# A gated feed-forward layer on one core: both first x blocks in one transfer, and the transposing transfer behind two gate loads

## The chip, the cores and the metric

The kernel runs on one core of a Trainium2 chip. Times are microseconds of device time for one execution. The engines are TensorE (PE; PEld is its loading of weights), VectorE (DVE), ScalarE (ACT), GpSimd (POOL) and SyncE (SP). SP and ACT issue the DMA transfers, each on a queue of its own, and 16 DMA engines carry them out.

## The reference

```python
def reference(x, w_gate, w_up, w_down):
    return (_gelu(x @ w_gate) * (x @ w_up)) @ w_down
```

`x` is [32, 32, 1024] in bf16, so 1024 tokens of 1024 features; `w_gate` and `w_up` are [1024, 3584], `w_down` is [3584, 1024], all bf16, and `_gelu` is the tanh approximation.

## The kernel before

The kernel computes each of its large products in two halves of every dimension, with Strassen's scheme (Winograd's form): seven products of sub-matrices in place of eight, at the price of sums and differences that VectorE and GpSimd form. In the first phase the left operand is the pair (gate, up), cut by feature half: `a11` and `a12` are the gate's rows for the features 0 to 511 and 512 to 1023, `a21` and `a22` those of up. The right operand is x transposed, cut by feature half and token half: `b11`, `b12` (features 0 to 511, first and second 512 tokens), `b21`, `b22` (features 512 to 1023). Each of these tiles is 128 partitions by 4 blocks (`KD` = 4, a block k is 128 features) by 512 tokens. The second phase multiplies the result by `w_down` in the same way; the change doesn't touch it.

The products with `t1` to `t4` (differences of the b tiles) and `s1` to `s4` (sums of weight tiles) need many tiles before they can begin. The kernel therefore opens with products that need little: gate rows `a12` by `b21`, for the first 24 of 28 column blocks of 128 (`NAHEAD` = 24), in six groups of four (`KB` = 4). The gate rows of groups 0 and 1 go to the tiles `a12a`, those of groups 2 to 5 to the tiles `a12b`; one 128x512 product has four matmuls, k = 0 to 3. Its result is copied out of the accumulators to `ahead`.

The whole is written under a manual schedule: each engine and each queue does its work in the order of the program text, and semaphores hold an instruction until what it needs is there. A transfer also waits, on its issuing engine, until the transfer eight places before it in the program has landed, since eight semaphores are used in turn. So the order of the lines is the order of the queues.

For the change, the opening matters. `b21` must be filled with transposed x. Its blocks k = 0 and 1 come the quick way: x is loaded as it lies, into `x_nat` (`load_nat`, L200), TensorE transposes it by 128x128 blocks into accumulator tiles `tp` (L267), and a copy takes each `tp`, half of the tokens of one block, to `b21` (L270). Its blocks k = 2 and 3 come by a transposing DMA transfer, `load_xT` (L220). In the kernel before, the order of the transfers is:

- SP: `x_nat` block 0; gate row k = 0 of group 0; gate row k = 1 of group 0; the transposing transfer of `b21` blocks 2 and 3; gate rows 2 and 3 of group 0; of group 1; the `a12b` rows of groups 2 and 3; `wu` and `wg` of the first chunk of weights; the rows of group 4; `b11`; `b12`; and so on.
- ACT: a tiny load of gate values, `probe` (L209); `x_nat` block 1; gate rows 0 and 1 of group 1. Behind these ACT loads its activation table.

The order on TensorE is: six matmuls on constants (L259, `NWARM`), the four transposes of x block 0, four short matmuls on constants (L274, `NFILL`), then the products (L289). Group 0 with k = 0 is done for the first half of the tokens; then x block 1 is transposed; then k = 0 for the second half, k = 1 for the first and the second, all these as 16 matmuls of 256 columns. Group 1 with k = 0 and 1 follows (8 matmuls of 512 columns), then k = 2 and 3 of group 0 and of group 1, then the groups 2 to 5 and the rest of the kernel.

Of the kernel before, what the change touches and what calls it, by code (L numbers as in the profile page):

```python
# [13 lines left out]
def kernel(  # L14
# [20 lines left out]
    nc = tc.nc  # L35
    P = nc.NUM_PARTITIONS
# [6 lines left out]
    xf = x.flatten_outer_dims()  # L43
# [5 lines left out]
    DT, FT = D // P, F // P  # L49
    KD = DT // 2  # L50
# [4 lines left out]
    KQ = DT // 4  # L55
# [4 lines left out]
    KB = 4  # L60
# [47 lines left out]
    def acc(tag):  # L108
        return ps1.tile([P, NB], fp32, name=f"ps{tag}", tag=tag, bufs=BANKS[tag])
# [5 lines left out]
    b21 = xpool.tile([P, KD, NB], bf16, name="b21")  # L115
# [8 lines left out]
    ahead_at = [t[:, k, :] for t in ahead for k in range(t.shape[1])]  # L124
# [38 lines left out]
    def sums(ci, *engs):  # L163

        a11, a12, a21, a22 = quads(ci)
        s1, s2, s4, s3 = (
            spool.tile([P, KD, FC * P], f32r, name=n, tag=n)[:, :, : len(chunks[ci]) * P]
            for n in ("s1", "s2", "s4", "s3")
        )
        s_tiles[ci] = (s1, s2, s3, s4)  # L170
        yield engs[0].tensor_tensor(s1, a21, a22, ADD)  # L171
        yield engs[1].tensor_tensor(s2, s1, a11, SUB)  # L172
        yield engs[2].tensor_tensor(s4, a12, s2, SUB)  # L173
        yield engs[3].tensor_tensor(s3, a11, a21, SUB)  # L174
# [17 lines left out]
    NB_P = NB // P  # L192
    probe = xpool.tile([P // 8, KQ, 2], bf16, name="probe")
    nc.gpsimd.memset(probe, 0.0)  # L194
    HALF = NB_P // 2
    x_nat = spool.tile([P, NB_P, KQ * P], bf16, name="x_nat", tag="s1")

    with tc.manual_schedule():
        def load_nat(eng, dt, p0, p1):
            eng.dma_start(  # L200
                out=x_nat[:, p0:p1, dt * P : (dt + 1) * P],
                in_=xf[p0 * P : p1 * P, (KD + dt) * P : (KD + dt + 1) * P].rearrange("(b p) d -> p b d", p=P),
            )

        assert KQ == 2
        load_nat(nc.sync, 0, 0, NB_P)


        nc.scalar.dma_start(out=probe, in_=wg_r[::8, KD : KD + KQ, :2])  # L209

        def load_ahead(i, k0, k1, eng=nc.sync, j0=0, j1=KB):
            f0 = i * KB
            eng.dma_start(
                out=a12_ahead[i][:, k0:k1, j0 * P : j1 * P],
                in_=wg_r[:, KD + k0 : KD + k1, (f0 + j0) * P : (f0 + j1) * P],
            )

        def load_xT(nb, d0, d1):
            t = ((b11, b12), (b21, b22))[d0 // KD][nb]
            nc.sync.dma_start_transpose(  # L220
                out=t[:, d0 % KD : (d1 - 1) % KD + 1, :], in_=xf[nb * NB : (nb + 1) * NB, d0 * P : d1 * P]
            )

        load_ahead(0, 0, 1)
        load_nat(nc.scalar, 1, 0, NB_P)
        load_ahead(0, 1, 2)
        load_xT(0, KD + KQ, DT)
        load_ahead(1, 0, KQ, nc.scalar)
        a12_ahead += [spool.tile([P, KD, KB * P], bf16, name="a12b", tag=t) for t in ("s2", "s4", "s1", "s3")]
        for i in (0, 1):  # L230
            load_ahead(i, KQ, KD)
        def load_halves(i):
            for k in range(0, KD, KQ):
                load_ahead(i, k, k + KQ)

        load_halves(2)
        load_halves(3)
        for which in (1, 0):
            load_w_all(0, which)
# [20 lines left out]

        tps = [[ps1.tile([P, HALF * P], bf16, name="tp", tag="A", bufs=BANKS["A"]) for _ in range(2)] for _ in range(KQ)]

        def transposed(dt):
            for half, tp in enumerate(tps[dt]):
                p0 = half * HALF
                for b in range(HALF):
                    nc.tensor.transpose(  # L267
                        tp[:, b * P : (b + 1) * P], x_nat[:, p0 + b, dt * P : (dt + 1) * P], ident
                    )
                nc.vector.tensor_copy(b21[:, dt, p0 * P : (p0 + HALF) * P], tp)  # L270

        transposed(0)
        for _ in range(NFILL):
            nc.tensor.matmul(warm_ps[:, :P], lhsT=ones_w, rhs=ones_w, start=True, stop=True)  # L274

# [11 lines left out]
        def product_ahead(ps, i, j, k0=0, k1=KD, cols=slice(None)):  # L287
            for k in range(k0, k1):
                nc.tensor.matmul(  # L289
                    ps[:, cols],  # L290
                    lhsT=a12_ahead[i][:, k, j * P : (j + 1) * P],
                    rhs=b21[:, k, cols],
                    start=(k == 0 and not cols.start),
                    stop=(k == KD - 1),
                    skip_group_check=True,
                )

        def group_ahead(i, tags, copies=(nc.scalar.copy,), between=None):
            for j, tag in enumerate(tags):
                if between and 2 * j == KB:  # L300
                    between()
                ps = acc(tag)
                product_ahead(ps, i, j)
                copies[j % len(copies)](ahead_at[i * KB + j], ps)
# [22 lines left out]

        both = (nc.scalar.copy, nc.vector.tensor_copy)  # L330
        ps = [[acc(t) for t in tags] for tags in ("CCAA", "AAAA")]
        for k in range(KQ):
            for half in range(2):
                for j in range(KB):
                    product_ahead(ps[0][j], 0, j, k, k + 1, slice(half * HALF * P, (half + 1) * HALF * P))
                if k == half == 0:
                    transposed(1)
        for j in range(KB):
            product_ahead(ps[1][j], 1, j, 0, KQ)
        for i in (0, 1):  # L340
            for j in range(KB):
                product_ahead(ps[i][j], i, j, KQ)
                both[j % 2](ahead_at[i * KB + j], ps[i][j])
        group_ahead(2, "CCAA", both)
        group_ahead(3, "AAAA", both)
        chunk0 = sums(0, *[nc.gpsimd] * 3, nc.vector)
        for _ in range(3):
            next(chunk0)
# [241 lines left out]
        for h0, h1, upto in ((0, NB - P, NB // 2), (NB - P, NB, NB)):  # L590
            cols = slice(h0, h1)
            ps = acc("C")[:, : h1 - h0]
# [33 lines left out]
```

## Time and profile before

| what | value |
|---|---|
| time, median of three runs | 274.2 us (273.19, 274.2, 274.35) |
| span of the profiled execution, first to last instruction | 271.9 us |
| TensorE busy | 267.5 us, 98% |
| VectorE busy | 204.0 us, 75% |
| ScalarE busy | 115.5 us, 42% |
| GpSimd busy | 119.7 us, 44% |
| moved by DMA | 35.86 MB, mean 132 GB/s |
| granted TensorE clock, mean | 1.000 |

The profiled execution's own time is given by its span; the profile states no other time for it. The span leaves out what lies before the first and after the last instruction, so it is compared with spans, and the median with medians. In the profile, a group of instructions is named by its line, its engine, and "written tile<-read tiles"; numbers behind an arrow in square brackets are the idle time before it and what ended it. "Time to landing" of a transfer runs from the start of its issue to its last signal of completion.

### The profile page before, as it was taken

What the parts mean: (1) busy time and instruction counts of PE and PEld (TensorE: products, weight loads), DVE (VectorE), ACT (ScalarE), POOL (GpSimd) and SP (SyncE); (2) the same over time, 40 slices, a digit from 0 to 9 for tenths busy, and PEclk for the clock granted to TensorE, in tenths of its full rate; (3) what the DMA queues carried; (4) which work ended last, traced back from release to release, by engine and by line L of the source; (5) the groups of instructions that cost most, each with busy time, mean ns of one, the idle gap of its engine ahead of it and who ended that gap; (6) DMA issues with size and microseconds to landing.
All of it is one profiled execution on the core that took longest, in us unless ns stands there. A gap on an engine that the chain in (4) does not pass through costs nothing.

```text
span 271.9 us, 3424 instructions
## 1 busy us (share of the span) xinstructions
PE 267.5 (98%) x1216; PEld 192.9 (71%) x1216; DVE 204.0 (75%) x205; ACT 115.5 (42%) x189; POOL 119.7 (44%) x61
## 2 busy tenths in 40 slices
PE   7999999999999999999999999999999999999995
PEld 4444776886787688688688687764458888888883
DVE  1447998986976877876777478469999999998621
ACT  2335756545644653645636535434000307870000
POOL 1090089986994995995995987000000000000000
PEclk9999999999999999999999999999999999999999
DMA  6999321504505505415234190005981437774111
GB/s 162 328 237 233 84 78 39 158 25 130 157 0 154 155 2 154 121 33 157 69 88 120 43 333 9 0 2 189 359 262 60 164 106 261 260 214 156 66 50 58
DMA packets 56576, 35.86 MB, mean 132 GB/s; under 512 B 9840, under 2 KB 56560, under 8 KB 56560
## 3 DMA queue, kind: packets, MB, share of 16 engines
q1 hardware_dynamic: 53264, 33.17, 43.0%
q10 hardware_dynamic: 3296, 2.49, 2.8%
q8 instruction: 9, 0.15, 0.2%
q14 instruction: 7, 0.06, 0.1%
HBM read 31.72 MB, written 2.10 MB: 124 GB/s over the span
## 4 chain that ended last, share of the span: by engine, by line
PE 97%; DMA 1%; POOL 0%; issue 0%; DVE 0%; ACTq 0%; POOLq 0%
PE psA L278 38%; PE psA L430 24%; PE psC L278 19%; PE psC L430 7%; PE psA L289 5%; PE psC L289 2%; DMA x_nat<-in_x_dram 1%; PE psC L594 1%; PE tp L267 0%; POOL ident masks.py:199 0%; DVE o_last L595 0%; POOL probe L194 0%; ACTq L209 0%; POOL ident masks.py:197 0%; POOLq L610 0%
## 5 line engine op out<-in xcount | busy, mean ns | idle before, releaser
L278 PE MATMUL psA<-t,s 128*128 128x512 f32 x224 | 57.3, 397 | 0.0
L251 ACT ACTIVATE h<-c 128x512 bf16<-128x512 f32 x56 | 34.6, 629 | 41.4 <-DVE c L308 41.4
L278 PEld LDWEIGHTS psA<-t,s 128*128 128x128 f32 x224 | 42.1, 188 | 9.5
L171 POOL TENSOR_TENSOR s<-wu 128x1024 fp32r<-128x1024 bf16 x13 | 28.9, 2224 | 31.4 <-DMA wu<-in_w_up_dram 30.7
L172 POOL TENSOR_TENSOR s<-s,wg 128x1024 fp32r<-128x1024 f32 x14 | 32.0, 2286 | 15.3 <-DVE s L171 14.3
L278 PE MATMUL psA<-b,wg 128*128 128x512 bf16 x128 | 29.4, 380 | 0.0
L174 POOL TENSOR_TENSOR s<-wg,wu 128x1024 fp32r<-128x1024 bf16 x13 | 28.4, 2187 | 0.0
L278 PE MATMUL psA<-t,a22r 128*128 128x512 f32 x112 | 27.9, 391 | 0.0
L278 PE MATMUL psC<-t,s 128*128 128x512 f32 x112 | 27.9, 391 | 0.0
L278 PE MATMUL psC<-b22r,s 128*128 128x512 f32 x112 | 27.7, 389 | 0.0
L308 DVE TENSOR_TENSOR c<-sn,psA 128x512 f32<-128x512 f32 x32 | 21.8, 682 | 6.7 <-PE psA L278 5.9
L313 ACT COPY sn<-psC 128x512 f32<-128x512 f32 x28 | 16.3, 588 | 22.9 <-PE psC L278 15.2
L278 PEld LDWEIGHTS psC<-t,s 128*128 128x128 f32 x112 | 21.0, 188 | 4.5
L278 PEld LDWEIGHTS psA<-t,a22r 128*128 128x128 f32 x112 | 21.0, 188 | 4.5
L278 PEld LDWEIGHTS psC<-b22r,s 128*128 128x128 f32 x112 | 21.0, 188 | 4.4
L308 DVE TENSOR_TENSOR c<-sn,psC 128x512 f32<-128x512 f32 x28 | 19.2, 687 | 6.2 <-PE psC L278 6.2
L407 DVE TENSOR_TENSOR lo<-c,h 128x512 bf16<-128x512 f32 x14 | 22.5, 1608 | 0.9
L278 PEld LDWEIGHTS <-wg 128*128 128x128 bf16 x128 | 11.8, 98 | 15.3 <-issue 2.4
L173 POOL TENSOR_TENSOR s<-wg,s 128x1024 fp32r<-128x1024 bf16 x10 | 21.6, 2158 | 0.8
L313 ACT COPY sn<-psA 128x512 f32<-128x512 f32 x32 | 18.3, 592 | 4.9 <-PE psA L278 4.7
L308 DVE TENSOR_TENSOR c<-ahead,psA 128x512 f32<-128x512 f32 x24 | 16.4, 687 | 3.9 <-PE psA L278 2.3
L326 DVE TENSOR_TENSOR hi<-h,psA 128x512 bf16<-128x512 bf16 x14 | 9.6, 688 | 11.3 <-PE psA L278 11.3
(88 smaller groups left out, 381.0 us busy)
## 6 DMA issues: line engine op xcount, KB each, us to landing
wu<-in_w_up_dram SPq DMA_DIRECT2D x14, 512.0 KB, 4.0
wdb<-in_w_down_dram SPq DMA_DIRECT2D x12, 512.0 KB, 4.8
wg<-in_w_gate_dram SPq DMA_DIRECT2D x9, 512.0 KB, 5.3
wdb<-in_w_down_dram SPq DMA_DIRECT2D x12, 384.0 KB, 4.6
v<-in_w_down_dram SPq DMA_DIRECT2D x4, 512.0 KB, 6.4
out_dram<-o_sb ACTq DMA_DIRECT2D x15, 128.0 KB, 1.7
a12b<-in_w_gate_dram SPq DMA_DIRECT2D x6, 256.0 KB, 5.1
wg<-in_w_gate_dram SPq DMA_DIRECT2D x6, 256.0 KB, 4.7
```

Of the source, the lines that this page charges most:

```text
L171: yield engs[0].tensor_tensor(s1, a21, a22, ADD)
L172: yield engs[1].tensor_tensor(s2, s1, a11, SUB)
L173: yield engs[2].tensor_tensor(s4, a12, s2, SUB)
L174: yield engs[3].tensor_tensor(s3, a11, a21, SUB)
L251: nc.scalar.activation(h, src, ACT.Gelu_apprx_tanh)
L278: nc.tensor.matmul(ps, lhsT=lhs[:, k, :], rhs=rhs[:, k, :], start=(start and k == 0), stop=(k == KD - 1), skip_group_check=True,)
L289: nc.tensor.matmul(ps[:, cols], lhsT=a12_ahead[i][:, k, j * P : (j + 1) * P], rhs=b21[:, k, cols], start=(k == 0 and not cols.start), stop ...
L308: tt(t, s, ps, ADD)
L313: nc.scalar.copy(t, ps)
L326: tt(g_of(ft)[:, :NB], h0, psa, MUL)
L407: tt(g_of(ft)[:, NB:], added(sn5[fl], psa[fl]), h1[fl], MUL)
L430: nc.tensor.matmul(banks[m], lhsT=lhs(k)[:, m * P : (m + 1) * P], rhs=rhs(k), start=(start and k == 0), stop=(k == HF - 1), skip_group_che ...
```

## The change

One transfer on SP now loads both x blocks, in rows of 256 features rather than 128. ACT's queue, from which the second x block goes, takes the gate row k = 1 of group 0 in its place. On SP the transposing transfer of `b21` blocks 2 and 3 stands behind gate rows 2 and 3 of groups 0 and 1 instead of ahead of them. TensorE transposes both x blocks, eight 128x128 blocks, before the four short matmuls, and the products of group 0 are no longer broken by the second block's transposes. Of the four copies out of `tp`, those of the second half of the tokens go from VectorE to ScalarE. The copies of the products stay on the engines that they had; only the pair of names is in the other order.

```diff
-        def load_nat(eng, dt, p0, p1):
+        def load_nat(eng, p0, p1):
             eng.dma_start(
-                out=x_nat[:, p0:p1, dt * P : (dt + 1) * P],
-                in_=xf[p0 * P : p1 * P, (KD + dt) * P : (KD + dt + 1) * P].rearrange("(b p) d -> p b d", p=P),
+                out=x_nat[:, p0:p1, :],
+                in_=xf[p0 * P : p1 * P, KD * P : (KD + KQ) * P].rearrange("(b p) d -> p b d", p=P),
             )
 
         assert KQ == 2
-        load_nat(nc.sync, 0, 0, NB_P)
+        load_nat(nc.sync, 0, NB_P)
...
         load_ahead(0, 0, 1)
-        load_nat(nc.scalar, 1, 0, NB_P)
-        load_ahead(0, 1, 2)
-        load_xT(0, KD + KQ, DT)
+        load_ahead(0, 1, 2, nc.scalar)
         load_ahead(1, 0, KQ, nc.scalar)
         a12_ahead += [spool.tile([P, KD, KB * P], bf16, name="a12b", tag=t) for t in ("s2", "s4", "s1", "s3")]
         for i in (0, 1):
             load_ahead(i, KQ, KD)
+        load_xT(0, KD + KQ, DT)
+
...
+        both = (nc.vector.tensor_copy, nc.scalar.copy)
+
         def transposed(dt):
             for half, tp in enumerate(tps[dt]):
...
-                nc.vector.tensor_copy(b21[:, dt, p0 * P : (p0 + HALF) * P], tp)
-
-        transposed(0)
+                both[half](b21[:, dt, p0 * P : (p0 + HALF) * P], tp)
+
+        for dt in range(KQ):
+            transposed(dt)
...
-        both = (nc.scalar.copy, nc.vector.tensor_copy)
         ps = [[acc(t) for t in tags] for tags in ("CCAA", "AAAA")]
         for k in range(KQ):
             for half in range(2):
                 for j in range(KB):
                     product_ahead(ps[0][j], 0, j, k, k + 1, slice(half * HALF * P, (half + 1) * HALF * P))
-                if k == half == 0:
-                    transposed(1)
...
                 product_ahead(ps[i][j], i, j, KQ)
-                both[j % 2](ahead_at[i * KB + j], ps[i][j])
-        group_ahead(2, "CCAA", both)
-        group_ahead(3, "AAAA", both)
+                both[(j + 1) % 2](ahead_at[i * KB + j], ps[i][j])
+        group_ahead(2, "CCAA", both[::-1])
+        group_ahead(3, "AAAA", both[::-1])
```

## The prediction

> **What bounds the kernel now.** I read the page first, then the chain that ended last in order of time, then the timeline of the first 16 us, the transfers' times to landing, and the stretches of the opening. The page says who is busy:
>
> ```profile
> span 271.9 us, 3424 instructions
> PE 267.5 (98%) x1216; PEld 192.9 (71%) x1216; DVE 204.0 (75%) x205; ACT 115.5 (42%) x189; POOL 119.7 (44%) x61
> ...
> PE 97%; DMA 1%; POOL 0%; issue 0%; DVE 0%; ACTq 0%; POOLq 0%
> ```
>
> TensorE has 4.4 us of the span in which it does nothing, and the chain in order of time is TensorE from start to end but for one transfer:
>
> ```profile
> 1.42 4.04 DMA x_nat<-in_x_dram
> 5.46 0.04 issue
> 5.51 0.40 PE tp L267 x4
> 5.91 0.22 PE psC L289 x2
> ```
>
> From 5.51 us on, TensorE runs without a gap to the last matmuls at 269 us. So the change can win or lose only by shifting this stream at its head, or by tearing a hole in it. The timeline of the head:
>
> ```profile
> 0.78 2.72 PE L259 MATMUL psA<-const-bfloat16-1.0 128*128 128x512 bf16 x6 [0.78 <-PEq L610]
> ...
> 2.25 1.34 SPq L220 DMA_TRANSPOSE b<-in_x_dram  x1
> ...
> 2.46 1.28 ACT L251 ACT_TABLE_LOAD   x1 [2.46 <-issue]
> ...
> 3.29 0.61 PE L267 MATMUL tp<-ident,x_nat 128*128 128x128 bf16 x4
> ...
> 3.72 0.41 PE L274 MATMUL psA<-const-bfloat16-1.0 128*128 128x128 bf16 x4
> 3.75 0.49 DVE L270 COPY b<-tp 128x256 bf16<-128x256 bf16 x2 [3.75 <-PE tp L267]
> ...
> 4.82 0.39 PE L289 MATMUL psC<-b,a12a 128*128 128x256 bf16 x2 [0.68 <-DMA a12a<-in_w_gate_dram]
> ...
> 8.78 1.03 PE L289 MATMUL psC<-b,a12a 128*128 128x512 bf16 x4
> ```
>
> Products start at 4.82, when the first gate row of group 0 has landed; they pause from 5.27 to 5.51 for the second x block; at 8.78 begins the stage that needs the blocks of the transposing transfer (k = 2, 3). That start is my measuring point, because nothing holds the stream behind it. It stands 8.78 us into the span only by TensorE's own work: the transfers it needs had landed. Their landings, as issue plus time to landing: first x block 0.74 + 2.2 = 2.9; gate row k=0 of group 0, 1.24 + 3.5 = 4.8; second x block 1.42 + 4.0 = 5.4; gate row k=1, 1.78 + 3.9 = 5.7; rows 0, 1 of group 1, 1.91 + 4.5 = 6.4; transposing transfer 2.25 + 5.1 = 7.3; rows 2, 3 of group 0, 3.64 + 4.7 = 8.3; of group 1, 4.26 + 4.8 = 9.0. The last four are needed at 7.05, 8.78, 8.78 and 10.5. The stretches of the opening show that the DMA engines, not the issuing queues, space these landings:
>
> ```profile
> 1.75:2.50 0.75, 0.75 (x4) 0.21 (x2) 0.00 (x0) 0.04 (x1) 0.00 (x0) 1.00 0.81 182
> 2.50:3.60 1.10, 1.10 (x6) 0.50 (x5) 0.00 (x0) 1.10 (x1) 0.00 (x0) 1.00 0.46 93
> ...
> 4.00:5.00 1.00, 0.32 (x5) 0.17 (x3) 0.23 (x2) 0.00 (x0) 0.00 (x0) 1.00 1.15 343
> ...
> 7.50:9.50 2.00, 2.00 (x11) 0.94 (x10) 0.00 (x0) 0.09 (x1) 0.00 (x0) 1.00 1.10 353
> 11.50:13.00 1.50, 1.50 (x9) 0.69 (x7) 1.26 (x2) 0.81 (x2) 0.00 (x0) 1.00 1.20 295
> ...
> 17.40:19.00 1.60, 1.60 (x9) 0.76 (x8) 0.69 (x1) 0.52 (x1) 1.52 (x2) 1.00 1.24 101
> ```
>
> The last two columns are DMA share and GB/s: from 4 us on they are full (343 to 353 with 1 KB rows, 295 with 512 B rows), with a hollow of 93 between 2.5 and 3.6, and a second one of 101 around 18 us, in which the transposing transfer of b11 was under way.
>
> **The change part by part.** Durations are from this execution; its span of 271.9 lies 2.3 below the median of the runs, 274.2, and I take that difference as unchanged.
>
> x in one transfer: 256 KB in rows of 512 B instead of 128 KB in rows of 256 B, issued by SP at the same 0.74. The first block's data flowed from 1.75 to 2.5 at 182 GB/s and landed 0.45 later. Low end: as many rows, so the same 2.95. High end: the 4.0 us that the second block took from issue, 4.74. At 295 GB/s its 262,144 bytes take 0.89, 0.14 more than now; part of the 0.75 was ramp, and the hollow at 2.5 begins inside it, so I take 3.3. The low end is nearer, because the transfer is still first on its queue.
>
> The Trainium skill (DMA: Bandwidth & Descriptors, Specifications) asks for 512 B per row for line rate. By that rule x would cost 262,144 bytes at the measured 353 GB/s, 0.74 us, and land at 2.95; the row of 512 B transfers here, 295 against 353 with 1 KB, speaks for a smaller benefit.
>
> TensorE's head: the six warming matmuls end their issue at 3.3; eight transposes instead of four now stand before the four fills. Four took 3.29 to 3.72 (107 ns apart), the second four of before 5.51 to 5.74 (56 ns apart). Added 0.23 to 0.43 before the first product, removed 0.23 in the midst of the products: fills end at 4.2 to 4.4 instead of 3.97, beside the wait for the gate row. The pause of 0.24 at 5.27 goes.
>
> Copies of tp: of four on VectorE (0.28 each), two move to ScalarE. ScalarE is busy with its table load and one activation until 3.97, so its first copy can't begin earlier; it has no row of this shape; between 0.28 and the 0.59 of its 128x512 copy I take 0.35. Its copies end at 4.3 and 4.7 (latest 5.15), needed at 0.43 and 1.3 after the first product: hidden if that is at 4.4 (4.83 and 5.7), and late by up to 0.05 otherwise. VectorE's two end at 4.05 and 4.4. Nothing else waits behind them: ScalarE's next work is at 9.41, VectorE's at 9.85.
>
> Gate row k=0, still SP's second transfer: now behind twice the bytes of x on its own queue, but without x's second block beside it on ScalarE's. Bounds 4.2 (half of the hollow goes) and 5.1 (0.35 later, as x); I take 4.4, nearer to now. It starts the products; k=1 moves from SP to ScalarE's queue, in the place of the second x block (1.42), lands between 4.7 and 5.4 and is needed at 5.27. Rows 0, 1 of group 1 keep their place behind as many bytes on that queue: 6.4 again. Needed at 4.4 + 16 x 0.109 = 6.14, so a new wait of 0.3 takes the place of the old pauses; then 8 x 0.216 = 1.73, and the k = 2 stage could start at 8.2.
>
> The transposing transfer moves past two loads of 256 KB on SP's queue, whose issues (0.57 and 0.46) now precede its own 1.34. SP would issue it about 2.8 to 4.2 instead of 2.25 to 3.59; the row loads behind it waited on SP for the second x block until 5.46 (0.2 of wait) and now don't. What sets its landing is the bytes: before, 1,536 KB (x 256, gate rows 1,024, transposed 256) had landed at 9.04, with rows 2, 3 of group 1 last. The same bytes now end with the transposed ones. Savings: 512 rows fewer, worth 0.15 at most (0.47 for 131 KB at 277 to 287 GB/s against 0.37 at 353, and rounding up), and half of the 0.6 us left idle in the hollow (share 0.46 over 1.1 us), 0.3. So 9.04 - 0.45 = 8.6. Low end 8.2, where the group 1 rows bind instead; high end 9.04 plus what a transposing transfer lost around 18 us, 1.6 x (1 - 101/285) = 1.03, so 10.1. The forecast is nearest to 9.04, the landing that it takes the place of.
>
> Rows 2, 3 of group 0 land earlier (about 7.2 instead of 8.3), those of group 1 at about 7.8, when nothing needs them: their cover was never short. The groups behind (a12b, wu, wg, b11) come behind the same bytes as before: first a12b 9.8 against a need at 12.2, a12b of group 4 at 16.3 against 19.1, b11 at 19.5 against 22.8. GpSimd issues none of the moved transfers; its first sum waits for wu (to 14.0), unmoved.
>
> Sum: the k = 2 stage starts at 8.6 instead of 8.78, so -0.2; I add nothing for the rest. Span 271.7, and 274.2 - 0.2 = 274.0 on the runs' scale.
>
> **The rivals.**
> 1. The transposed blocks are in time: with the hollow gone they land by 8.2, and the wait for group 1's rows, or none, decides: start at 7.9 to 8.2, -0.6 to -0.9, 273.3 to 273.6. For it: 0.6 us of idle DMA before 3.6. Against: full share from 4 us on.
> 2. The transposing transfer stalls, as b11's did at 17.4:19.0 (101 GB/s between 287 before and 277 after), now with TensorE waiting: landing 9.1 to 10.1, +0.3 to +1.3, 274.5 to 275.5. Before, its own packets also slowed (144 GB/s in 5.5:6.2), which was hidden.
> 3. The other side: TensorE's speed-up slips. Matmuls were 0.43 apart (512 columns) from 0.78 and double speed came at about 3.75, 2.97 later, in the middle of unbroken work. If x lands at 4.74, TensorE idles 1.4 us from 3.3; should the 2.97 then count anew, double speed comes at 7.7. Eight transposes (0.86), four fills (0.43): products from 6.0, eight at 0.213 to 7.7, eight at 0.109 to 8.6, then 1.73: start at 10.3, +1.5, 275.7. It decides only if x lands some 0.5 us or more behind the warming matmuls.
>
> The Trainium skill (TensorE: Matmul & The Clock Gate, Part 1) says the clock opens after a busy window of about 3.4 us that runs free of the kernel, so that the moment varies from run to run. The 2.97 here fits that; by the page the slip could also befall the kernel before, which waits 0.7 us at 4.1.
>
> **How the numbers follow.** The forecast (start at 8.2 to 9.0, 273.6 to 274.4) has 0.52, rival 1 0.15, rival 2 0.18, rival 3 0.10; 0.05 is left for what I don't see. The runs of before alone spread over 1.16 us, so about 0.5% (1.37 us) is what can be told from no change. Faster by more needs a start before 7.4, which the landing at 8.2 excludes short of chance: 0.05. Slower by more: rival 3, the top of rival 2 with the runs' spread on it, and some of the unseen, 0.17. Within: 0.78. The range takes in rival 1 with 0.2 of spread, and reaches through rival 2: 273.1 to 275.5.
>
> **What would show it.** Right: x landing near 3.3, products from about 4.4, no pause for a second x block, a wait of TensorE at the k = 2 matmuls released by the transposing transfer, that stage beginning 8.2 to 9.0, and the stream unbroken after it. Wrong: products at or after 4.8; a wait at group 1's rows longer than 0.5; transposes or products still at half speed after 4.5; the k = 2 stage past 9.1; any new TensorE wait behind 10 us.

## The result, and the profile after

The changed kernel takes 274.64 us (median of 20 runs, 273.85 to 275.34), the kernel before 274.06 (20 runs): a ratio of 1.0028, with a 95% interval of 1.0018 to 1.0038. That is 0.6 to 0.8 us slower; the forecast was 0.2 us faster. The size lies within the 0.5% that the forecast called too little to tell from no change, and inside its range; the interval lies wholly above 1, and the direction is wrong.

The page of the changed kernel, and its chain in order of time:

```profile
span 272.4 us, 3421 instructions
...
PE 268.0 (98%) x1216; PEld 193.2 (71%) x1216; DVE 202.0 (74%) x203; ACT 116.5 (43%) x191; POOL 119.6 (44%) x61
...
PE 96%; DMA 2%; ACTq 0%; POOL 0%; issue 0%; DVE 0%; POOLq 0%
```

```profile
1.43 0.44 ACTq L213
1.87 0.03 issue
1.90 5.69 DMA a12a<-in_w_gate_dram
7.59 0.05 issue
7.64 1.90 PE psA L292 x8
9.54 0.65 PE psC L292 x3
```

The span is 0.5 longer. One transfer still stands at the head of the chain, but it is another one: no longer the second x block, landing at 5.46, but the gate rows 0 and 1 of group 1, which ScalarE's queue issues at 1.90 and which land at 7.59. From 7.64 on TensorE runs without a gap. The timeline of the head (start, duration, and in brackets the idle time before and what ended it):

```profile
2.76 1.34 SPq L220 DMA_TRANSPOSE b<-in_x_dram  x1
3.57 0.77 PEld L269 LDWEIGHTS <-x_nat 128*128 128x128 bf16 x8 [0.99 <-DMA x_nat<-in_x_dram]
3.58 1.03 PE L269 MATMUL tp<-ident,x_nat 128*128 128x128 bf16 x8
...
4.41 0.63 PE L277 MATMUL psA<-const-bfloat16-1.0 128*128 128x128 bf16 x4
...
4.83 0.54 PE L292 MATMUL psC<-b,a12a 128*128 128x256 bf16 x2
...
6.52 0.38 PE L292 MATMUL psA<-b,a12a 128*128 128x256 bf16 x2
...
7.64 1.90 PE L292 MATMUL psA<-b,a12a 128*128 128x512 bf16 x8 [0.74 <-DMA a12a<-in_w_gate_dram]
...
9.38 1.03 PE L292 MATMUL psC<-b,a12a 128*128 128x512 bf16 x4
```

The products start at 4.83, as before (4.82). The break for the second x block is gone, so the 16 short matmuls end their issue at 6.73 instead of 7.05, 0.3 sooner. Then TensorE stands for 0.9 (from 6.73 to 7.64; the 0.74 in brackets counts from the end of the last matmul, not of its issue) where it stood not at all before, and the k = 2 stage starts at 9.38 instead of 8.78: +0.6, the whole of the longer span. The transposing transfer, on which the forecast had put the wait, landed at 9.28 (issued at 2.76) and was in time by only 0.1.

The stretches of the opening of the changed kernel (the last two columns are DMA share and GB/s; the share is the summed time of the packets over the time of the 16 engines, so it can exceed 1):

```profile
2.50:3.60 1.10, 1.02 (x4) 0.11 (x3) 0.00 (x0) 1.10 (x1) 0.00 (x0) 1.00 1.10 336
3.60:4.00 0.40, 0.40 (x5) 0.40 (x6) 0.00 (x0) 0.28 (x2) 0.00 (x0) 1.00 0.73 223
4.00:5.00 1.00, 1.00 (x11) 0.98 (x10) 0.58 (x2) 0.73 (x2) 0.00 (x0) 1.00 0.70 186
5.00:5.50 0.50, 0.50 (x6) 0.42 (x4) 0.00 (x0) 0.02 (x1) 0.00 (x0) 1.00 0.79 266
...
6.70:7.50 0.80, 0.20 (x2) 0.00 (x0) 0.00 (x0) 0.00 (x0) 0.00 (x0) 1.00 1.46 155
7.50:8.50 1.00, 0.86 (x4) 0.40 (x5) 0.00 (x0) 0.00 (x0) 0.00 (x0) 1.00 0.79 160
```

The hollow in the DMA engines, 93 GB/s and a share of 0.46 at 2.5 to 3.6 before, is not filled. It is shallower now and lies between 3.6 and 5.5 (186 to 266 GB/s, shares of 0.70 to 0.79), where the engines were at 343 before, and so it falls on other transfers. The low rates at 6.7 to 8.5 come while the transposing packets run (803 of 884 packets there are under 512 B); up to 7.5 the engines are busy in them, with a share of 1.46.

The completion signals in the trace say more than the one landing time. Before, the first of the 16 DMA engines was done with rows 0 and 1 of group 1 at 6.29 and the last at 6.44. In the changed kernel the first was done at 5.61, and the last at 7.59. TensorE's next product began at 7.64, after the last of the 16.

The trace also tells the bytes apart by queue. From 4.0 to 5.5, ScalarE's queue moved 0.32 MB in the kernel before and 0.16 MB in the changed one, SP's queue 0.19 and 0.16. From 5.5 to 7.5, SP's queue moved 0.41 MB in the changed kernel beside the last 0.11 of ScalarE's. So group 1's rows do take turns with what SP issued, but the hollow fell on them as well, and how much of the delay is due to each is not told apart here.

### The profile page after: what moved, and what is told of

It is laid out like the page before. It is cut to its first block, busy times and chain, and to the rows that moved or that the text cites. A ratio compares the mean times of both kernels' runs of the same rounds, so it can differ in the third digit from the quotient of the medians.

```text
span 272.4 us, 3421 instructions
## 1 busy us (share of the span) xinstructions
PE 268.0 (98%) x1216; PEld 193.2 (71%) x1216; DVE 202.0 (74%) x203; ACT 116.5 (43%) x191; POOL 119.6 (44%) x61
## 4 chain that ended last, share of the span: by engine, by line
PE 96%; DMA 2%; ACTq 0%; POOL 0%; issue 0%; DVE 0%; POOLq 0%
PE psA L281 38%; PE psA L430 24%; PE psC L281 19%; PE psC L430 7%; PE psA L292 5%; PE psC L292 2%; DMA a12a<-in_w_gate_dram 2%; PE psC L594 1%; ACTq L213 0%; POOL ident masks.py:199 0%; DVE o_last L595 0%; POOL probe L194 0%; ACTq L209 0%; POOL ident masks.py:197 0%; POOLq L610 0%
## 5 line engine op out<-in xcount | busy, mean ns | idle before, releaser
L407 DVE TENSOR_TENSOR lo<-c,h 128x512 bf16<-128x512 f32 x14 | 21.3, 1525 | 0.9
```

Source lines behind the costliest of these rows:

```text
L407: tt(g_of(ft)[:, NB:], added(sn5[fl], psa[fl]), h1[fl], MUL)
```

## The experiments

Three theories were set against each other. A: the transposing transfer, late in the queue, holds up its neighbours. B: the hollow belongs to the first reads of the gate matrix. C, formed after the first four runs: the order of the loads is at fault, because the rows 0 and 1 of group 1, on ScalarE's queue, share the DMA engines with the rows 2 and 3, which SP now issues at 1.8 and 2.3 instead of 3.6 and 4.3 (those of group 0 thus ahead of group 1's rows, which ScalarE issues at 1.9). A fourth, H, concerns the speed of TensorE.

**The transposing transfer back in its place.**

```diff
         load_ahead(0, 0, 1)
+        load_xT(0, KD + KQ, DT)
         load_ahead(0, 1, 2, nc.scalar)
...
             load_ahead(i, KQ, KD)
-        load_xT(0, KD + KQ, DT)
```

> The changed kernel with the transposing transfer back in its old place, right behind gate row k=0 of group 0; everything else of the change stays. Theory A (the transposing transfer, being issued or carried out, takes the DMA engines from whatever is behind it or beside it, and in the changed kernel this falls on rows 0 and 1 of group 1): the hollow in the DMA engines comes back to about 2.5 to 3.6 us, rows 0 and 1 of group 1 land by 6.8 instead of 7.6, TensorE's pause at 6.7 goes from 0.9 us to 0.2 or less, and the k = 2 stage starts at 8.4 to 8.7 instead of 9.38: ratio to before 0.997 to 1.000. Theory B (the hollow belongs to the first reads of the gate matrix, whoever is issuing): the rows still land after 7.3, the k = 2 stage starts at 9.1 or later, ratio 1.002 to 1.003.

Measured: 1.0002 (0.9984 to 1.0020), so this one line gives the loss back. The timeline:

```profile
6.83 2.11 PE L292 MATMUL psA<-b,a12a 128*128 128x256 bf16 x10
...
8.77 1.03 PE L292 MATMUL psC<-b,a12a 128*128 128x512 bf16 x4
```

No pause is left: rows 0 and 1 of group 1 landed at 6.75 (6.35 on the first engine), and the k = 2 stage starts where it did before. All spans but one of 12 are 271.4 to 272.2, against 272.1 to 273.5 in the 20 runs of the changed kernel. (The profiled execution is the one exception, at 273.5. Its last matmul starts at 268.72, as before, so its excess lies behind TensorE's work.) The DMA hollow did not move to where theory A wanted it: there are 334 GB/s at 2.5 to 3.6. The 170 at 3.75 to 5.5 are no idle time (share 1.21; 306 of 525 packets are under 512 B, as those of the transposing transfer are); the engines have idle time at 5.5 to 6.2 (share 0.56, 116 GB/s). So a hollow ahead of the landing of group 1's rows does not by itself cost the time. The edit also brings the transposed blocks forward, from 9.28 to 7.70, so this run takes away both waits at once.

**That move alone, in the kernel before.**

```diff
-        load_xT(0, KD + KQ, DT)
         load_ahead(1, 0, KQ, nc.scalar)
...
             load_ahead(i, KQ, KD)
+        load_xT(0, KD + KQ, DT)
```

> The kernel before with only the transposing transfer moved behind rows 2 and 3 of groups 0 and 1; x still comes in two transfers. Theory A: rows 0 and 1 of group 1 land later than the 6.4 of before, about 7.3 to 7.8, TensorE pauses at 7.05 for 0.3 to 0.8 us, the k = 2 stage starts at 9.1 to 9.6 instead of 8.78, ratio 1.001 to 1.003: the move alone carries the loss. Theory B: the rows land at 6.4 as before, and the loss of the changed kernel comes from the single x transfer and TensorE's head; the k = 2 stage starts at 8.8 to 8.9, ratio 0.999 to 1.001.

Measured: 1.0002 (0.9979 to 1.0025). Group 1's rows landed later, at 7.03, in A's direction but short of its 7.3, and again with a spread between the engines (from 5.50), but TensorE, still broken by the second x block, needed them only at 6.93, and the k = 2 stage started at 8.85. Its median span is 272.05, against 271.8 of the kernel before in the same session. So, by the median spans, the move costs about a quarter of a microsecond without the single x transfer (the interval, up to 1.0025, does not exclude more), and the single x transfer costs nothing that can be told without the move; most of the loss needs both. The hollow of this execution, which still loads x in two transfers, lay early, as before: 82 GB/s at 3.0 to 3.5, and 336 from 5.0 to 5.5. It was over before group 1's rows were needed, which fits the small loss but does not prove that it is the reason.

**A plain load in the place of the transposing one.**

```diff
-        load_xT(0, KD + KQ, DT)
+        nc.sync.dma_start(
+            out=b21[:, KQ:, :].rearrange("p k t -> p (k t)").rearrange("p (b d) -> p b d", b=NB_P),
+            in_=xf[:NB, (KD + KQ) * P : DT * P].rearrange("(b p) d -> p b d", p=P),
+        )
```

> The changed kernel with the transposing transfer of b21 blocks 2 and 3 replaced, in the same place, by a plain load of the same 256 KB (512 rows of 512 B), so blocks 2 and 3 of b21 hold untransposed x. Theory A: without a transposing transfer there the DMA engines stay full between 3.75 and 8 us, rows 0 and 1 of group 1 land by 6.2 and the plain load by 7.5; no pause of TensorE over 0.2 at 6.7, k = 2 stage at 8.5. Theory B: the share between 3.75 and 5.5 stays at 0.6 to 0.8 and the rows land after 7.

Measured: 1.0030 (1.0007 to 1.0052). With no transposing transfer at this place the loss is there all the same, which speaks against A. The median span is 272.5, and the profiled execution is the fastest of the eight (271.8), with its k = 2 stage at 8.76, so its trace does not show where the others lost their time. Even in that one rows 0 and 1 of group 1 needed until 6.97, with the first engine done at 5.54, and the first products waited for the gate row of group 0:

```profile
5.11 0.39 PE L295 MATMUL psC<-b,a12a 128*128 128x256 bf16 x2 [0.60 <-DMA a12a<-in_w_gate_dram]
...
8.76 1.03 PE L295 MATMUL psC<-b,a12a 128*128 128x512 bf16 x4
```

Neither theory has its numbers here: the rows came after A's 6.2, but just ahead of B's 7, and the engines' share between 3.75 and 5.5 was 0.94, above B's 0.6 to 0.8. The plain load landed at 8.60.

**Seven warming matmuls.** The edit is `NWARM = 7`.

> The changed kernel with seven warming matmuls instead of six, so that TensorE has no 0.28 us of idle time before x lands at 3.5. Theory H (that idle time put off TensorE's double speed from 3.75 to 5.05): transposes from 3.72 on are 56 ns apart, products start at 4.5 or before instead of 4.83. Rival (the moment is set by something that runs free of the kernel): spacing of 107 ns until about 5, products at 4.95. Either way group 1's rows decide later: k = 2 stage at 9.3 to 9.5, ratio 1.002 to 1.004.

Measured: 1.0027 (1.0010 to 1.0044). With no idle time before the transposes, TensorE kept half speed until 6.3 (256-column matmuls 0.21 apart up to there, 0.11 after), later than in the changed kernel. So H falls in this form: unbroken work from 0.78 on did not bring double speed at 3.75. Group 1's rows landed at 8.1 and decided again: the k = 2 stage started at 9.88, later than the 9.3 to 9.5 expected.

**Group 1's rows on SP's queue, ahead of rows 2 and 3.**

```diff
-        load_ahead(1, 0, KQ, nc.scalar)
+        load_ahead(1, 0, KQ)
```

> The changed kernel with rows 0 and 1 of group 1 loaded by SP, ahead of rows 2 and 3 of both groups, instead of by ScalarE's queue beside them; the transposing transfer stays late. Theory C (the loss comes from order: on the DMA engines the rows of group 1 take turns with the rows 2 and 3 that SP now issues 1.9 us earlier, so their slowest engine ends at 7.0 to 8.1 instead of 6.4): on one queue the rows land by 6.6, within 0.6 us of each other, TensorE's pause at 6.7 is 0.2 or less, and the next wait is for the transposed blocks at 9.2, so the k = 2 stage starts at 8.6 to 9.3, last matmuls 0.1 to 0.6 before the changed kernel's 269.36; ratio 0.999 to 1.002. Theory A (a late transposing transfer as such is the cause): rows land after 7, pause 0.5 or more, ratio 1.002 to 1.004.

Measured: 1.0011 (0.9993 to 1.0029). The interval alone excludes neither no loss nor the whole of it; the median span is 272.1 against 271.9 of the kernel before in that session. The timeline:

```profile
6.58 2.11 PE L292 MATMUL psA<-b,a12a 128*128 128x256 bf16 x10
...
8.97 1.02 PE L292 MATMUL psC<-b,a12a 128*128 128x512 bf16 x4 [0.28 <-DMA b<-in_x_dram]
```

The rows landed at 6.46 and the pause before them is gone, although the transposing transfer is still late. The spread between the engines was larger than C expected (from 4.90). Now the next wait shows: the k = 2 stage stands for the transposed blocks, which landed at 8.93. This is the wait that the forecast had described; it stood behind the longer one at group 1's rows.

**No short matmuls before the products.** The edit is `NFILL = 0`.

> The changed kernel without the four short matmuls before the first product. Theory C: the products start 0.2 to 0.43 earlier, at 4.4 to 4.6, but the rows of group 1 decide, so the pause before them grows by as much and the k = 2 stage starts when it did, 9.3 to 9.5; ratio 1.002 to 1.004. Theory H (the longer head of TensorE, eight transposes and the fills at half speed, is what was lost): the k = 2 stage starts at 9.0 or before, ratio 1.001 or less.

Measured: 1.0026 (1.0011 to 1.0041). Products began at 4.61, and the pause took the gain:

```profile
8.23 1.90 PE L292 MATMUL psA<-b,a12a 128*128 128x512 bf16 x8 [1.00 <-DMA a12a<-in_w_gate_dram]
...
9.97 0.59 PE L292 MATMUL psC<-b,a12a 128*128 128x512 bf16 x2
```

The rows landed at 8.18 in this execution, and the median span is 272.75, against the 271.9 of the kernel before. What TensorE does ahead of them isn't what was lost. The k = 2 stage, at 9.97, was later than expected by 0.5, with the rows.

**One queue in the order of need.** SP loads x, row 0 of group 0, rows 0 and 1 of group 1, then transposes, then loads rows 2 and 3.

```diff
         load_ahead(0, 1, 2, nc.scalar)
-        load_ahead(1, 0, KQ, nc.scalar)
+        load_ahead(1, 0, KQ)
+        load_xT(0, KD + KQ, DT)
...
             load_ahead(i, KQ, KD)
-        load_xT(0, KD + KQ, DT)
```

> The changed kernel with one queue in the order of need: SP loads x, row 0 of group 0, rows 0 and 1 of group 1, then the transposing transfer, then rows 2 and 3; ScalarE loads row 1 of group 0. Theory C: group 1's rows land by 6.2, the transposed blocks by 7.7, rows 2 and 3 of group 0 by 8.3; no pause over 0.2, k = 2 stage at 8.3 to 8.6, ratio 0.997 to 1.000. Theory A: as early a transposing transfer gives the same as in the run with it behind row 0, 8.77 and 1.000; rows after it.

Measured: 1.0004 (0.9987 to 1.0022), median span 271.85 against 271.9 of the kernel before in that session. The rows landed at 5.92, and in the profiled execution the k = 2 stage started sooner than in any other:

```profile
4.63 0.38 PE L292 MATMUL psC<-b,a12a 128*128 128x256 bf16 x2
...
6.16 2.11 PE L292 MATMUL psA<-b,a12a 128*128 128x256 bf16 x10
...
8.10 1.03 PE L292 MATMUL psC<-b,a12a 128*128 128x512 bf16 x4
```

That execution is the fastest of its twelve (271.2) and had TensorE at double speed early; over the runs it is no faster than the kernel before.

**Second executions.** Both kernels were profiled once more, unchanged.

> The changed kernel once more, for a second execution in the records. Theory C: rows 0 and 1 of group 1 again come with a spread of over 1.5 us between the first and the last DMA engine and end after 7.2; the k = 2 stage starts at 9.2 or later; the moment of TensorE's double speed is another than 5.05, without changing that.

> The kernel before once more, for a second execution in the records. Theory C: rows 0 and 1 of group 1 again land within 0.5 us of each other and before 6.9; no pause of TensorE over 0.2 after 6 us; the k = 2 stage at 8.7 to 9.1, whatever the moment of double speed.

The changed kernel: rows 0 and 1 of group 1 at 7.05, not after 7.2, with a spread of 1.0, not 1.5; the k = 2 stage at 8.83, the span 271.9. Double speed came at about 5.5, another moment, as expected. It is a lucky execution, below all 20 spans of the timed runs, and shows how far the landing varies: 7.05, 7.59, and in the two runs that changed only TensorE's head 8.1 and 8.18. The kernel before: rows at 6.29 (first engine 6.14), as expected, the k = 2 stage at 8.94, the span 272.0.

**Half of the rows in front.** The transposing transfer stands between rows 2, 3 of group 0 and rows 2, 3 of group 1.

```diff
-        for i in (0, 1):
-            load_ahead(i, KQ, KD)
-        load_xT(0, KD + KQ, DT)
+        load_ahead(0, KQ, KD)
+        load_xT(0, KD + KQ, DT)
+        load_ahead(1, KQ, KD)
```

> The changed kernel with the transposing transfer between rows 2, 3 of group 0 and rows 2, 3 of group 1 on SP: half of the bytes that took turns with rows 0 and 1 of group 1 now come behind it. Theory C: the rows land between the two orders, 6.6 to 7.3, TensorE's pause is 0.5 or less, the k = 2 stage at 8.6 to 9.0; ratio 0.999 to 1.002. If the amount in front does not matter: rows at 7.0 to 8.2 as in the changed kernel, ratio 1.002 to 1.004.

Measured: 1.0013 (0.9997 to 1.0029), median span 272.25 (271.9 for the kernel before), between the two orders as C says. But in the profiled execution, which has the longest span of its ten (272.7), the rows landed only at 7.87 (on the first engine at 7.64), not at 6.6 to 7.3, and TensorE was at half speed until about 6.6:

```profile
7.92 1.90 PE L292 MATMUL psA<-b,a12a 128*128 128x512 bf16 x8 [0.17 <-DMA a12a<-in_w_gate_dram]
...
9.65 0.81 PE L292 MATMUL psC<-b,a12a 128*128 128x512 bf16 x3
```

The time is in the middle, the landing isn't. So how much stands in front is not the only thing that sets the landing, and this run does not settle the share.

## Why the prediction was wrong

**The step that failed** is "Rows 0, 1 of group 1 keep their place behind as many bytes on that queue: 6.4 again." The bytes ahead of them on ScalarE's queue were indeed the same. But the landing does not go by that queue alone. In the kernel before, SP spent 2.25 to 3.59 on issuing the transposing transfer and only then issued rows 2 and 3, at 3.64 and 4.26. In the changed kernel these 512 KB were issued by 2.7, the first half of them at 1.78, ahead of group 1's rows at 1.90, and shared the DMA engines with them. Of these the forecast had noted only that they "land earlier (about 7.2 instead of 8.3), those of group 1 at about 7.8, when nothing needs them" (7.4 and 8.2 were measured). What they took was not free: group 1's rows landed at 7.59 in the profiled execution. Instead of a new wait of 0.3, TensorE had one of 0.9, and the k = 2 stage started at 9.38, past the forecast's own sign of being wrong (9.1). Taking the two loads apart, by putting group 1's rows first on one queue, removed the wait (6.46 and 5.92, no pause), and so did putting the transposing transfer ahead of rows 2 and 3 (6.75, no pause). That the order of the loads costs the time is shown by these runs; how it does so is not wholly known, since with half of the rows behind the transposing transfer the landing was still 7.87 in the one execution with a trace.

The Trainium skill (DMA: Bandwidth & Descriptors, Issuing engines are not separate DMA queues) says just this: transfers issued from SP and from ScalarE run on the same 16 DMA engines and interleave. The rows' landing at 7.59 instead of 6.44, with as many bytes ahead on their own queue, agrees.

**The transposing transfer** was expected at 8.6, the decisive wait; it landed at 9.28, in the upper half of the bounds (8.2 to 10.1). This term was mis-sized by 0.7. The forecast had taken 0.45 off the 9.04 at which the same bytes had landed before, for fewer rows and half of the hollow; instead 0.24 was added, and the hollow, which moved, was not halved. It wasn't decisive in the profiled execution, because TensorE came later still, but only by 0.1: had group 1's rows come at 6.4 with all else as measured, the k = 2 stage would have started at about 9.3, 0.5 later than before and not 0.2 sooner. When the wait ahead of it was removed, it did decide: blocks at 8.93, a wait of 0.28, the stage at 8.97. The mechanism was right and stood second; its size alone would have turned the sign in this execution.

**x in one transfer** landed at 3.53 against 3.3; the gate row k = 0 at 1.24 + 2.8 = 4.0 against 4.4. Still products started at 4.83, not 4.4: the eight transposes and four fills, which the forecast had ending at 4.2 to 4.4, nearly all ran 107 ns apart, since double speed came only at about 5.05. That is rival 3 in a small form. Its price could not be charged to the change, though. In its second execution the kernel before, too, reached double speed only after 5.7, and its k = 2 stage started 0.16 later than in the first. And in the run without fills, products 0.2 sooner did not win the loss back (1.0026).

The Trainium skill (TensorE: Matmul & The Clock Gate, Part 1) says that the window which opens the clock runs free of the kernel. The moments here, 3.75 and about 5.7 in two executions of one kernel, and 6.3 with unbroken work from 0.78 on, agree with that and not with a count that starts with the work. The shortest time to double speed, 2.97 us from the first matmul, is less than the busy window of about 3.4 us that the Trainium skill gives there, so the forecast's "fits" holds only roughly.

**The copies** on ScalarE ended at 5.02 and were never waited for; nothing behind the opening waited anew. These points stood as written.

**Rival 2** had the right sign and the right size (+0.3 to +1.3), and its landing (9.1 to 10.1) came true at 9.28, with 155 to 160 GB/s while the transposing packets ran. But TensorE was not waiting for it, and with a plain load in its place the loss stayed (1.0030), so a slow transposing transfer is not the whole reason.

Open remains why the DMA engines have a hollow between 2.5 and 6 us, and why some engines come out of it up to 2 us after others. Taken in steps of half a us, six of seven executions had 55 to 184 GB/s in its deepest step, at 3.0 to 3.5 us with x in two transfers and between 3.5 and 5.5 with x in one. The seventh is the run in the order of need: it held 261 GB/s or more up to 5.0, and its 116 at 5.0 to 5.5 fell on busy engines (share 1.30). The hollow is there with a plain load in place of the transposing one (164 at 3.5 to 4.0), so that transfer is not its only cause; that the first reads of the gate matrix make it (theory B) was not tried by itself.

## What to carry to other kernels

Here a load that was brought forward "when nothing needs it" was paid for by the load that was needed next, though that one stood on another queue. When a queue's order is changed, go through every transfer that is issued from any queue before the first needed landing, not just those ahead on the same queue. Then price the wait that stands second, too: here it ended 0.1 before the first, and in the run that took the first away it was the one that decided. An instruction that occupies an issuing queue for 1.3 us may be what spaces the loads well; where it is moved, ask what the queue will do in that time.

## What was unexpected

The gate rows of group 1 landed anywhere between 7.05 and 8.18 in four executions whose transfers were the same (two of them with TensorE's head changed), while in the order of before they came at 6.29 and 6.44. The order seems to change how much the landing scatters, not only when it comes; two executions of the one and four of the other are too few to show it. The second profile of the changed kernel alone (span 271.9) would have shown no loss at all; the medians of many runs were needed.
